# A cross network on one Trainium2 core: a semaphore lane for each transposed input tile, and the second layer's weights loaded behind the second group's rows

## Chip, cores and metric

The kernel runs on one core of a Trainium2 chip. The metric is the device time of one execution in microseconds (us); lower is better. The kernel before takes 488.22 us (median of 6 runs).

## The reference

```python
B, F, D, L = 16384, 26, 16, 6          # Din = F * D = 416; everything is bfloat16
def reference(x0, ws, bs):             # x0 [B, 416], ws [6, 416, 416], bs [6, 416]
    x = x0
    for l in range(L):
        x = x0 * (x @ ws[l] + bs[l]) + x
    return x
```

## The kernel before

The rows are cut into 8 groups of 2048. A group is held transposed, with features on the partitions: three tiles of 128 features (`t` = 0 to 2) and a "tail" of 32 features, which is loaded through a buffer `Tb` and copied from there to a place called `x03`. A job `(g, l)` is layer `l` of group `g`. It has three output tiles and a tail. For an output tile TensorE does 12 full matmuls (three input tiles, four chunks of 512 columns) and four short ones for the 32 tail features ("rows32"). ScalarE adds the bias, and VectorE multiplies by x0 and adds x.

Weights come in two parts: `wm` (384 rows) and `w3` (the last 32 rows, loaded four times to different partitions; the trace prints it as `w`, and I call the second layer's `w_1`). Nearly all these transfers are issued by SP, in the order of the program. Group 0 is not loaded by the transposing transfers but turned by TensorE, and its first layer (the "first job") runs while group 1 is loaded.

This is how a group is loaded; `lane` names the semaphore (the counter by which an engine learns that data has landed), and a reader of anything in a lane waits for the whole batch in it:

```python
def load_group(g):
    s = slot(g)
    rows = slice(g * GC, (g + 1) * GC)
    def turn(t):
        add("sp", lambda h: h.dma_start_transpose(
            x0s[s][:, t * GC:(t + 1) * GC], x0[rows, t * P:(t + 1) * P]),
            writes=[x0_tok(s, t, j) for j in range(NJ)], lane=f"x0_{s}", batch=g)
    turn(0)
    add("sp", lambda h: h.dma_start_transpose(Tb[:, :], x0[rows, D - P:D]), writes=["Tb"], lane="Tb", batch=g)
    turn(1)
    turn(2)
    for j in range(NJ):                                   # x03: copies out of Tb
        ...
# ... the start of the program
load_w3(0, "sp")
make_wbd(0)
load_wm(1, "sp")      # second layer's weights
load_w3(1, "sp")
load_group(1)         # second group's rows
load_wm(2, "sp")
load_w3(2, "sp")
```

And this is the order in which TensorE meets what was loaded, right after the first job:

```
first job (0,0), ending in its tails      -> VectorE later writes x3, the new tail of group 0
(1,0) tile 0: 12 full matmuls             needs tiles 0, 1, 2 of group 1, in this order
(1,0) tile 0: 4 short matmuls             needs x03 of group 1
(0,1) tile 0: 4 short matmuls             needs w_1 and x3      <- important below
(0,1) tile 0: 12 full matmuls             needs wm of layer 1
(1,0) tile 1, then the tails of (0,1) and (1,0)
```

Of the kernel before, what the change touches and what calls it, by code (L numbers as in the profile page):

```python
# [21 lines left out]
class Program:  # L22
# [12 lines left out]
    def add(self, eng, fn, reads=(), writes=(), lane=None, batch=None, hold=False, release=False):  # L35
        op = Op(eng, fn, lane, batch)
        deps = {}
        if eng == "pool":
            writes = list(writes) + ["pool"]
        for t in reads:  # L40
            w = self.writer.get(t)
            if w is not None:
                deps[id(w)] = (w, True)
        for t in writes:
            w = self.writer.get(t)
            if w is not None:
                deps[id(w)] = (w, True)
            for r in self.readers.get(t, ()):
                if id(r) not in deps:
                    deps[id(r)] = (r, False)  # L50
        for d, raw in deps.values():
            if d.lane is None and d.eng == eng and lane is None and (eng == "pe" or not raw):
                continue
            op.deps.append(d)
        for t in reads:
            self.readers.setdefault(t, []).append(op)
        for t in writes:
            self.writer[t] = op
            self.readers[t] = []
        if eng == "dve":  # L60
            if hold:
                self.flush()
                self.held = op
            else:
                self.queue[eng].append(op)
                if release:
                    self.flush()
        else:
            self.queue[eng].append(op)
        if lane is not None:  # L70
            batches = self.lanes.setdefault(lane, [])
            if not batches or batches[-1][0] != batch:
                batches.append((batch, []))
            batches[-1][1].append(op)
        return op
# [123 lines left out]
def bass_standalone__cross_network_dcn__recsys_kernel(  # L199
# [9 lines left out]
    NJ = 4  # L209
# [48 lines left out]
    def x0_tok(s, t, j):  # L258
        return ("x0", s, t, j)
# [7 lines left out]
    def slot(g):  # L267
        return g % NX0
# [12 lines left out]
    def load_wm(l, eng):  # L281
        add(eng, lambda h: h.dma_start(wm[l][:, :, :], ws[l, 0:NT * P, :].rearrange("(t p) f -> p t f", p=P)),
            writes=[("wm", l)], lane=f"wm{l}", batch=0)

    def load_w3(l, eng):
        for j in range(NJ):
            add(eng, lambda h, j=j: h.dma_start(w3[l][j * T32:(j + 1) * T32, :], ws[l, NT * P:D, :]),  # L287
                writes=[("w3", l, j)], lane=f"w3{l}", batch=0)

    def make_wbd(l):  # L290
        add("pool", lambda h: h.memset(wbd[l][:, :], 0.0), writes=[("wbd", l)])
        for j in range(NJ):
            q = slice(j * T32, (j + 1) * T32)
            add("pool", lambda h, q=q: h.tensor_copy(wbd[l][q, q], w3[l][q, NT * P:D]),  # L294
                reads=[("w3", l, j)], writes=[("wbd", l)])

    def load_group(g):
        s = slot(g)
        rows = slice(g * GC, (g + 1) * GC)
        def turn(t):  # L300
            add("sp", lambda h: h.dma_start_transpose(  # L301
                x0s[s][:, t * GC:(t + 1) * GC], x0[rows, t * P:(t + 1) * P]),
                writes=[x0_tok(s, t, j) for j in range(NJ)], lane=f"x0_{s}", batch=g)

        turn(0)
        add("sp", lambda h: h.dma_start_transpose(Tb[:, :], x0[rows, D - P:D]),  # L306
            writes=["Tb"], lane="Tb", batch=g)
        turn(1)
        turn(2)
        for j in range(NJ):  # L310
            q = slice(j * T32, (j + 1) * T32)
            add("sp", lambda h, q=q, j=j: h.dma_start(x0s[s][q, XW:XW + CH], Tb[P - T32:P, j * CH:(j + 1) * CH]),
                reads=["Tb"], writes=[("x03q", s, j)], lane=f"x03_{s}", batch=g)
# [26 lines left out]
    def done_with(g, l):  # L340
        users[(g, l)] = users.get((g, l), 0) + 1
        if users[(g, l)] < 2:
            return
        if l > 0:
            free_x.append(xset[(g, l)])
            free_3.append(xtail[(g, l)])
        if l == L - 1:
            output(g)
            if g == 3:
                load_last()  # L350
            if 4 < g + NX0 <= LAST:
                load_group(g + NX0)
# [136 lines left out]
        load_nat(j, 0, KK)  # L489
    load_w3(0, "sp")  # L490
    make_wbd(0)
    load_wm(1, "sp")
    load_w3(1, "sp")
    load_group(1)
    load_wm(2, "sp")
    load_w3(2, "sp")
    make_wbd(1)
# [165 lines left out]
    def start_job(g, l):  # L663
        started.add((g, l))
        xset[(g, l + 1)] = free_x.pop(0)
        if (g, l) in W_LOAD:
            load_wm(W_LOAD[(g, l)], "sp")
            load_w3(W_LOAD[(g, l)], "sp")
            make_wbd(W_LOAD[(g, l)])
        if (g, l) in G_LOAD:  # L670
            load_group(G_LOAD[(g, l)])
# [48 lines left out]
    g, l = LAST, L - 1  # L720
# [158 lines left out]
```

## Time and profile before

| | before |
|---|---|
| time, median of 6 runs | 488.22 us (488.06 to 488.44) |
| the profiled run | 488.65 us, span 486.5 us |
| TensorE busy | 472.3 us, 97% of the span |
| TensorE's largest wait for a load | 1.9 us, once, near 20.5 us |

The profile's page gives, for each engine, busy time, share of the span and number of instructions:

```profile
PE 472.3 (97%) x3199; PEld 202.7 (42%) x3253; DVE 407.2 (84%) x713; ACT 343.1 (71%) x372; POOL 16.4 (3%) x44
```

The view of waits of TensorE in the kernel before lists what ended its idle time: us in total, times, longest us. Two of its lines: (The second is the start-up, before TensorE has anything to work with.)

```profile
PE ps L423 <- DMA x<-in_x_dram: 1.9, 1, 1.9
PE ps L503 <- POOL ident L467: 1.8, 1, 1.8
```

The view has one more wait on a load, of 0.4 us near 7.6 us, so the wait of 1.9 us is nearly all there is to gain here. TensorE's own order of time, in the kernel before, shows where it lies. Columns: start in us, duration in us, engine, line, what is done, count, and in brackets the idle time before and what ended it. L453 ends the first tails, L423 are full matmuls, L435 the short ones, L448 the second tails.

```profile
20.07 0.39 PE L453 MATMUL ps<-x,wbd 128*32 128x512 bf16 x4
22.39 2.54 PE L423 MATMUL ps<-x,wm 128*128 128x512 bf16 x11 [1.93 <-DMA x<-in_x_dram]
24.86 0.61 PE L435 MATMUL ps<-x,w 32*128 32x512 bf16 x8
25.40 5.35 PE L423 MATMUL ps<-x,wm 128*128 128x512 bf16 x24
...
31.01 0.83 PE L448 MATMUL ps<-x,wm 128*32 128x512 bf16 x12
```

The chain of waits of the kernel before (start us, us, what) shows what held that load (pieces of 0.04 us between these, called `issue`, are left out here and below). `SPq` is the issuing of a transfer by SP; the landing is the `DMA` piece.

```profile
7.82 0.42 SPq L287
8.29 3.06 SPq L301
11.39 2.99 SPq L306
14.43 3.25 SPq L301
17.73 4.39 DMA x<-in_x_dram
```

Line L287 issues w_1, line L301 the three tiles of group 1, line L306 the buffer `Tb`. The last tile lands at 22.1 us (17.73 + 4.39). Tile 0 landed at 14.8 and tile 1 at 19.9 us (start of the issue plus the time to landing, of each transfer by itself), but with one lane TensorE can't tell.

### The profile page before, as it was taken

Reading aid. Unit: us, or ns where it says so; the run is one execution under the profiler, and the core shown is the slowest. Engines: PE = TensorE matmul, PEld = TensorE weight load, DVE = VectorE, ACT = ScalarE, POOL = GpSimd, SP = SyncE. Lnnn points to the kernel's source line nnn. Section 1 sums busy time; section 2 is a strip of 40 time slices with the busy share of each in tenths; the row PEclk is TensorE's granted clock in tenths of the full one; section 3 lists DMA queues with packets and bytes.
Section 4 is the critical chain, followed back from the end, with each engine's and each line's share of the span. In section 5 each row is a group of like instructions: output and inputs, shape, how many; then the busy total and the mean of one; then the engine's idle time right before and its main releaser. Section 6 shows DMA issues by size and latency. Waiting matters only on the chain.

```text
span 486.5 us, 8047 instructions
## 1 busy us (share of the span) xinstructions
PE 472.3 (97%) x3199; PEld 202.7 (42%) x3253; DVE 407.2 (84%) x713; ACT 343.1 (71%) x372; POOL 16.4 (3%) x44
## 2 busy tenths in 40 slices
PE   7899999999999999999999999999999999999996
PEld 6334444444444444444444444444444444444353
DVE  2878888888888888888889888988888888888887
ACT  4567777677677677766767767767777767777775
POOL 1033000000000000000000000000000000000000
PEclk9999999999999999999999999999999999999999
DMA  9897990000001397269209911850000137027277
GB/s 235 166 195 169 170 156 1 0 1 0 2 1 37 67 237 127 44 141 232 50 9 193 225 39 33 212 179 1 1 1 1 23 68 193 0 44 165 78 156 263
DMA packets 126249, 47.65 MB, mean 98 GB/s; under 512 B 107002, under 2 KB 124804, under 8 KB 126212
## 3 DMA queue, kind: packets, MB, share of 16 engines
q1 hardware_dynamic: 125656, 46.71, 43.5%
q8 instruction: 25, 0.41, 0.4%
q10 hardware_dynamic: 556, 0.43, 0.3%
q14 instruction: 12, 0.10, 0.1%
HBM read 5.97 MB, written 13.63 MB: 40 GB/s over the span
## 4 chain that ended last, share of the span: by engine, by line
PE 91%; SPq 3%; ACT 2%; issue 2%; DMA 1%; DVE 1%; DVEq 0%
PE ps L423 73%; PE ps L435 8%; PE ps L448 6%; PE ps L453 2%; PE ps L767 1%; SPq L301 1%; DMA x<-in_x_dram 1%; SPq L287 1%; ACT tw L382 1%; SPq L306 1%; ACT x L795 1%; SPq L478 0%; ACT x L759 0%; PE ps L778 0%; DVE x L396 0%
## 5 line engine op out<-in xcount | busy, mean ns | idle before, releaser
L382 ACT ACTIVATE tw<-ps,bias 128x1024 bf16<-128x1024 f32 (+1 forms) x295 | 299.8, 1071 | 128.9 <-PE ps L435 107.5
L423 PE MATMUL ps<-x,wm 128*128 128x512 bf16 x1638 | 371.9, 379 | 7.4 <-issue 3.7
L423 PEld LDWEIGHTS ps<-x,wm 128*128 128x128 bf16 x1692 | 158.9, 98 | 215.2 <-issue 28.3
L391 DVE TENSOR_TENSOR tw<-tw,x 128x1024 bf16<-128x1024 bf16 (+1 forms) x285 | 193.8, 686 | 63.9 <-ACT tw L382 63.6
L396 DVE TENSOR_TENSOR x<-tw,x 128x1024 bf16<-128x1024 bf16 (+1 forms) x285 | 182.3, 680 | 0.0
L435 PE MATMUL ps<-x,w 32*128 32x512 bf16 x564 | 44.3, 380 | 0.0
L448 PE MATMUL ps<-x,wm 128*32 128x512 bf16 x564 | 38.7, 380 | 0.0
L409 ACT ACTIVATE ts<-ps,bias 128x512 bf16<-128x512 f32 x47 | 28.8, 701 | 0.0
L435 PEld LDWEIGHTS ps<-x,w 32*128 32x128 bf16 x564 | 9.0, 92 | 33.1 <-issue 33.1
L448 PEld LDWEIGHTS ps<-x,wm 128*32 128x32 bf16 x564 | 13.8, 96 | 15.7 <-issue 2.9
L609 POOL COPY ost<-ot 128x512 bf16<-128x512 bf16 x7 | 4.8, 686 | 413.1 <-DMA ot<-x 413.1
L413 DVE TENSOR_TENSOR x<-ts,x 128x512 bf16<-128x512 bf16 x47 | 18.6, 420 | 0.0
L411 DVE TENSOR_TENSOR ts<-ts,x 128x512 bf16<-128x512 bf16 x47 | 18.6, 419 | 0.0
L453 PE MATMUL ps<-x,wbd 128*32 128x512 bf16 x188 | 18.3, 379 | 0.0
L294 POOL COPY wbd<-w 32x32 bf16<-32x32 bf16 x24 | 9.4, 392 | 35.9 <-DMA w<-in_ws_dram 34.7
L767 PE MATMUL ps<-wm,x 128*128 128x416 bf16 x48 | 9.4, 341 | 0.0
L536 DVE COPY x<-ps 128x512 bf16<-128x512 bf16 x4 | 1.7, 425 | 8.5 <-PE ps L528 8.5
L795 ACT ACTIVATE x<-ps 128x416 bf16<-128x416 f32 x15 | 7.4, 530 | 1.3 <-PE ps L767 1.2
L533 ACT ACTIVATE x<-ps 128x512 bf16<-128x512 bf16 x8 | 4.3, 594 | 4.6 <-PE ps L523 4.6
L453 PEld LDWEIGHTS ps<-x,wbd 128*32 128x32 bf16 x188 | 5.0, 97 | 5.1
L767 PEld LDWEIGHTS ps<-wm,x 128*128 128x128 bf16 x48 | 5.1, 115 | 3.8 <-issue 1.4
L797 DVE TENSOR_TENSOR x<-x,x 128x416 bf16<-128x416 bf16 x15 | 5.5, 371 | 1.1 <-ACT x L795 1.0
(37 smaller groups left out, 48.2 us busy)
## 6 DMA issues: line engine op xcount, KB each, us to landing
out_dram<-ost SPq DMA_DIRECT2D x7, 1664.0 KB, 6.8
x<-in_x_dram SPq DMA_DIRECT2D x7, 416.0 KB, 7.4
wm<-in_ws_dram SPq DMA_DIRECT2D x5, 312.0 KB, 3.2
x<-Tb SPq DMA_DIRECT2D x28, 32.0 KB, 2.2
out_dram<-x SPq DMA_DIRECT2D x1, 832.0 KB, 3.6
w<-in_ws_dram SPq DMA_DIRECT2D x24, 26.0 KB, 2.4
x<-in_x_dram SPq DMA_DIRECT2D x2, 208.0 KB, 3.1
out_dram<-x SPq DMA_DIRECT2D x1, 416.0 KB, 2.5
```

Source lines behind the costliest of these rows:

```text
L382: add("act", lambda h, a=a, w=w, b0=b0: h.activation(tw[r][:, a * CH:(a + w) * CH], psum[:, b0 * CH:(b0 + w) * CH], ACT_F.Identity, bias=b ...
L391: add("dve", lambda h, a=a, e=e: h.tensor_tensor(tw[r][:, a * CH:e * CH], tw[r][:, a * CH:e * CH], x0s[s0][:, i * GC + a * CH:i * GC + e * ...
L396: add("dve", lambda h, a=a, e=e: h.tensor_tensor(xs[so][:, i * GC + a * CH:i * GC + e * CH], tw[r][:, a * CH:e * CH], src(i, a, e), ALU.ad ...
L409: add("act", lambda h: h.activation(ts[r][:, :], bank(b), ACT_F.Identity, bias=bias[:, 3, l:l + 1], scale=1.0), reads=[("ps", b), "bias"], ...
L411: add("dve", lambda h: h.tensor_tensor(ts[r][:, :], ts[r][:, :], x0s[s0][:, XW:XW + CH], ALU.mult), reads=[("ts", r)] + x03_toks(s0), writ ...
L413: add("dve", lambda h: h.tensor_tensor(x3s[so][:, :], ts[r][:, :], src, ALU.add), reads=[("ts", r)] + stok, writes=[("x3", so)], hold=True)
L423: add("pe", lambda h, t=t, j=j: h.matmul(bank(banks[j]), wm[l][:, t, ecols], src(t, j, j + 1), start=(first and t == 0), stop=(not first a ...
L435: add("pe", lambda h, q=q, j=j: h.matmul(bank(banks[j]), w3[l][q, ecols], src[q, :], start=first, stop=not first, tile_position=(j * T32, 0)),
L448: add("pe", lambda h, t=t, j=j, src=src, l=l, b=b: h.matmul(bank(b, j * T32, (j + 1) * T32), wm[l][:, t, NT * P:D], src(t, j, j + 1), star ...
L453: add("pe", lambda h, j=j, s3=s3, l=l, b=b: h.matmul(bank(b, j * T32, (j + 1) * T32), wbd[l][:, j * T32:(j + 1) * T32], s3, start=False, s ...
L767: add("pe", lambda h, t=t: h.matmul(bank(b, n=D), xcol(t, j, kk), wm[l][:, t, :], start=(first and t == 0), stop=(not first and t == NT - 1)),
L795: add("act", lambda h: h.activation(o, bank(b, n=D), ACT_F.Copy), reads=[("ps", b)], writes=extra + [("on", j, kk)])
```

## The change

It has two parts. Each tile gets a lane of its own, so that TensorE can begin with tile 0 while tile 2 is on its way. And the second layer's weights no longer go ahead of the second group's rows: `wm` goes behind the three tiles and w_1 behind the x03 copies.

```diff
-    def load_group(g):
+    def load_group(g, between=lambda: None):
@@
-                writes=[x0_tok(s, t, j) for j in range(NJ)], lane=f"x0_{s}", batch=g)
+                writes=[x0_tok(s, t, j) for j in range(NJ)], lane=f"x0_{s}_{t}", batch=g)
@@
         turn(1)
         turn(2)
+        between()
@@
-    load_wm(1, "sp")
+    load_group(1, lambda: load_wm(1, "sp"))
     load_w3(1, "sp")
-    load_group(1)
     load_wm(2, "sp")
```

## The prediction

> **What bounds the kernel now.** The page's engine table gives TensorE 97% of a 486.5 us span, and the chain of waits is 91% TensorE. Its only large wait on a load is 1.9 us "PE ps L423 <- DMA x<-in_x_dram", once: from 20.46 us (end of the first tail, L453) to 22.39 us the first matmul of the second group waits. The chain of waits before that is SP's issue queue: row loads, first-layer tails, the second layer's weights (5.83, 0.49 us) and its four tail loads (6.37, 1.88 us), four transposes (8.29 to 20.05 us).
>
> The four transposes land (source-line view) at 14.8 (tile 0), 17.8 (Tb), 19.9 (tile 1) and 22.1 us (tile 2). With one lane of one batch, the first matmul waits for tile 2, though it needs only tile 0. The Trainium skill, "DMA: Bandwidth & Descriptors", section on why a DMA increments its semaphore by 16, says only a full count tells that all data landed; the old wait is therefore on all three.
>
> **What the change does.** (a) Lanes: tile 0 would be usable at once at 20.46; eight matmuls (0.22 us each) later, about 22.2, tile 2 has landed. This alone removes nearly the whole wait. (b) Order: about 2.46 us of issuing (0.53 + 1.92) moves from ahead of the transposes to behind them. Tile 2 should land near 19.7 to 20.3, before TensorE asks. Either part suffices; they aren't additive. No work is added or removed; a few more TensorE waits on full semaphores I count as nothing.
>
> **What it puts in the way.** The order view shows TensorE's next waits after the group's first 12 matmuls: the second group's tail rows (x03), then tail weights w_1 and, in the same wait, VectorE's x3 of the first job; then wm1.
> - TensorE reaches the x03 rows near 23.1, w_1/x3 near 23.35 (12 x 0.22 + 4 x 0.07 after 20.46). Before, the w_1 matmuls started near 25.15.
> - VectorE is busy without a gap from 16.9 to 24.33 us and writes x3 last (L413, 23.91 + 0.42). The removed wait doesn't gate it, so TensorE can't start the w_1 matmuls before about 24.4.
> - w_1 is now issued after x03, some 20.7 to 22.6 us, as SP's issuing in sum is unchanged; at 1.9 to 2.4 us to landing it arrives at 24.2 to 24.9. wm1 lands near 21.5, early enough.
>
> So of the 1.93 us about 1.2 to 1.6 returns as a new wait at L435 on w_1 or x3, and 0.3 to 0.75 us is gained. From then on TensorE is bound (59.2 to 59.4 of each 60 us), loads have over 5 us of slack, and the gain should carry to the end unchanged.
>
> **Predicted:** 487.75 us (gain 0.6), 8 in 10 range 487.0 to 488.4. Faster by over 2%: 0.005; within 2%: 0.99; slower by over 2%: 0.005.
>
> **What would show it.** Right: the wait at 20.46 is gone, x_1's matmuls start by 20.7; a new TensorE wait of 1 to 1.5 us stands before the w_1 matmuls of L435, ended by VectorE's L413 or the w_1 load at 24.4 to 24.9; wait list without the 1.9 us; from 60 us on all is shifted by a constant 0.3 to 0.75 us. Wrong: no such wait and a shift of about 1.9 us; or transposes that land no earlier.
>
> **What would make it wrong.** Transposes issued at 5.83 may meet the first group's loads still in flight (DMA share 1.02 in 6 to 9 us) and delay the first job, eating the gain; SP's issue of transposes may be held by a full queue (3.06 us for the first, against 1.89 us at 27.6), pushing w_1 past 25.1 and the gain to zero.

## The result, and the profile after

The changed kernel took 487.94 us (median of 6, 487.71 to 488.44) against 488.22 us. The ratio is 0.9995, with a 95% interval of 0.9983 to 1.0008. The time was inside the predicted range. The gain isn't clear of noise.

The profiles differ more than the times do: span 485.8 against 486.5 us. One line was added, so L423 became L424, L435 became L436 and so on. Two lines of the waits of TensorE in the changed kernel:

```profile
PE ps L503 <- POOL ident L468: 1.8, 1, 1.8
PE ps L436 <- DMA w<-in_ws_dram: 1.1, 1, 1.1
```

The wait for the rows is gone, and there is a new one, for w_1. TensorE's order of time in the changed kernel shows it:

```profile
19.91 0.39 PE L454 MATMUL ps<-x,wbd 128*32 128x512 bf16 x4
20.45 2.54 PE L424 MATMUL ps<-x,wm 128*128 128x512 bf16 x11 [0.16 <-ACT tw L383]
22.93 0.39 PE L436 MATMUL ps<-x,w 32*128 32x512 bf16 x4
24.41 0.40 PE L436 MATMUL ps<-x,w 32*128 32x512 bf16 x4 [1.09 <-DMA w<-in_ws_dram]
24.74 5.35 PE L424 MATMUL ps<-x,wm 128*128 128x512 bf16 x24
...
30.35 0.83 PE L449 MATMUL ps<-x,wm 128*32 128x512 bf16 x12
```

TensorE starts on group 1 at 20.45 instead of 22.39 us, 1.94 us earlier, but reaches the second tails only 0.66 us earlier (30.35 against 31.01). And right behind the load stands VectorE. Its order of time in the changed kernel has x3 as its last instruction of the first job:

```profile
23.29 0.42 DVE L412 TENSOR_TENSOR ts<-ts,x 128x512 bf16<-128x512 bf16 x1
23.74 0.43 DVE L414 TENSOR_TENSOR x<-ts,x 128x512 bf16<-128x512 bf16 x1
```

The w_1 load landed at 24.27 us (22.61 + 1.66 in the chain of waits) and x3 was written at 24.17 us. Both are needed by the matmuls that began at 24.41 us.

The chain of waits of the changed kernel shows that the transposes were issued earlier, but not by as much as the loads taken away from ahead of them:

```profile
5.52 4.25 SPq L301
9.82 2.94 SPq L306
12.80 2.68 SPq L301
15.53 2.29 SPq L301
17.86 0.59 SPq L282
```

The first transpose now takes 4.25 us to issue, against 3.06 us before. It starts 2.77 us earlier and ends 1.58 us earlier (9.77 against 11.35).

### The profile page after: what moved, and what is told of

It is laid out like the page before. It is cut to its first block, busy times and chain, and to the rows that moved or that the text cites. A ratio compares the mean times of both kernels' runs of the same rounds, so it can differ in the third digit from the quotient of the medians.

```text
span 485.8 us, 8047 instructions
## 1 busy us (share of the span) xinstructions
PE 472.8 (97%) x3199; PEld 203.2 (42%) x3253; DVE 407.2 (84%) x713; ACT 343.2 (71%) x372; POOL 16.0 (3%) x44
## 4 chain that ended last, share of the span: by engine, by line
PE 91%; SPq 4%; ACT 2%; issue 2%; DVE 1%; DMA 0%; DVEq 0%
PE ps L424 73%; PE ps L436 8%; PE ps L449 6%; PE ps L454 2%; SPq L301 2%; PE ps L767 1%; SPq L287 1%; ACT tw L383 1%; SPq L306 1%; ACT x L795 1%; SPq L313 0%; SPq L479 0%; DMA w<-in_ws_dram 0%; ACT x L759 0%; PE ps L778 0%
## 5 line engine op out<-in xcount | busy, mean ns | idle before, releaser
L424 PE MATMUL ps<-x,wm 128*128 128x512 bf16 x1638 | 371.9, 379 | 5.6 <-issue 3.7
L424 PEld LDWEIGHTS ps<-x,wm 128*128 128x128 bf16 x1692 | 158.8, 98 | 213.3 <-issue 28.5
L436 PE MATMUL ps<-x,w 32*128 32x512 bf16 x564 | 44.5, 380 | 1.1 <-DMA w<-in_ws_dram 1.1
L436 PEld LDWEIGHTS ps<-x,w 32*128 32x128 bf16 x564 | 9.2, 92 | 34.5 <-issue 33.1
L454 PE MATMUL ps<-x,wbd 128*32 128x512 bf16 x188 | 18.3, 379 | 0.0
L454 PEld LDWEIGHTS ps<-x,wbd 128*32 128x32 bf16 x188 | 5.0, 97 | 5.1
```

The source lines that it names most:

```text
L424: add("pe", lambda h, t=t, j=j: h.matmul(bank(banks[j]), wm[l][:, t, ecols], src(t, j, j + 1), start=(first and t == 0), stop=(not first a ...
L436: add("pe", lambda h, q=q, j=j: h.matmul(bank(banks[j]), w3[l][q, ecols], src[q, :], start=first, stop=not first, tile_position=(j * T32, 0)),
L454: add("pe", lambda h, j=j, s3=s3, l=l, b=b: h.matmul(bank(b, j * T32, (j + 1) * T32), wbd[l][:, j * T32:(j + 1) * T32], s3, start=False, s ...
```

## The experiments

Before the single runs, one account that holds for all of them. In each profile I read three numbers from TensorE's order of time: when the first tails end (start plus duration of the L453 or L454 group, 20.07 + 0.39 = 20.46 us in the kernel before), when the second tails start (31.01 us), and the **stage** between them (10.55 us). The last column is the time of that same run less the start of the second tails.

| profiled run | time us | first tails end | second tails start | stage | rest |
|---|---|---|---|---|---|
| before, first profile | 488.65 | 20.46 | 31.01 | 10.55 | 457.64 |
| before, second (before_p2) | 487.61 | 20.15 | 30.01 | 9.86 | 457.60 |
| before, third (before_p3) | 489.85 | 19.70 | 32.22 | 12.52 | 457.63 |
| changed, first profile | 487.98 | 20.30 | 30.35 | 10.05 | 457.63 |
| changed, second (after_again) | 487.34 | 19.84 | 29.72 | 9.88 | 457.62 |
| changed, third (after_p3) | 487.69 | 20.22 | 30.09 | 9.87 | 457.60 |
| lanes_only | 487.80 | 20.31 | 30.18 | 9.87 | 457.62 |
| order_only | 487.88 | 20.42 | 30.28 | 9.86 | 457.60 |
| tails_early | 487.85 | 20.38 | 30.25 | 9.87 | 457.60 |
| rows_last | 486.96 | 20.33 | 29.33 | 9.00 | 457.63 |
| tile_swap | 486.75 | 20.36 | 29.14 | 8.78 | 457.61 |
| tile_swap_lanes | 487.28 | 20.87 | 29.65 | 8.78 | 457.63 |
| tile_swap_before | 487.24 | 20.85 | 29.63 | 8.78 | 457.61 |
| w1_later | 491.42 | 20.19 | 33.76 | 13.57 | 457.66 |

The rest is 457.60 to 457.66 us in all fourteen. So whatever these kernels differ in has happened by the second tails, and nothing is given back later. What remains is when the first job ends, which varies between runs of one and the same code (19.70, 20.15, 20.46 for the kernel before), and the stage.

**My theory:** after the load wait, x3 by VectorE and the w_1 load are the next things that TensorE needs, both near 24.2 us, so most of a shorter load wait comes back as a wait there. **Rivals:** that only one of the two parts of the change gains; that the late w_1 load alone is the new limit; that the wait of 1.9 us in the first profile is typical of the kernel before.

### lanes_only, order_only: one part of the change at a time

lanes_only is the kernel before with the lanes split; order_only is the changed kernel with `lane=f"x0_{s}"` again.

```diff
# lanes_only, against the kernel before
-                writes=[...], lane=f"x0_{s}", batch=g)
+                writes=[...], lane=f"x0_{s}_{t}", batch=g)
# order_only, against the changed kernel
-                writes=[...], lane=f"x0_{s}_{t}", batch=g)
+                writes=[...], lane=f"x0_{s}", batch=g)
```

> Kernel before with only the semaphore lanes split; issue order untouched. My theory (after the load wait, x3 by VectorE at about 24.2 to 24.4 us and the w_1 load are the next things TensorE needs, so either part alone gives the whole gain): TensorE starts on the second group by 20.7 us although tile 2 lands only near 22.1; a short wait for the x03 rows (last lands near 23.8 us) and one for x3 follow; the w_1 matmuls start at 24.4 to 24.6 us; span shorter than before by 0.5 to 0.75 us, level with the changed kernel within 0.2 us. Rival (the new load order is what gains): no gain, under 0.2 us.

> The changed kernel with one lane for all three tiles again, so only the order of loading changes. My theory: tile 2 lands near 20.5 us, within 0.2 us of when TensorE asks; w_1 matmuls start at 24.4 us as in the changed kernel; gain 0.5 to 0.75 us against before, so the two parts are not additive. Rival (lanes are what gains): the wait at 20.46 stays near 1.9 us, no gain.

In both, the wait for the rows is gone, and TensorE waits for VectorE's x3 instead. TensorE's order of time in lanes_only, and then in order_only:

```profile
20.24 2.76 PE L423 MATMUL ps<-x,wm 128*128 128x512 bf16 x12
22.93 0.40 PE L435 MATMUL ps<-x,w 32*128 32x512 bf16 x4
24.24 0.39 PE L435 MATMUL ps<-x,w 32*128 32x512 bf16 x4 [0.91 <-DVE x L413]
```

```profile
20.35 2.76 PE L424 MATMUL ps<-x,wm 128*128 128x512 bf16 x12
23.04 0.40 PE L436 MATMUL ps<-x,w 32*128 32x512 bf16 x4
24.34 0.40 PE L436 MATMUL ps<-x,w 32*128 32x512 bf16 x4 [0.91 <-DVE x L414]
```

The stage is 9.87 and 9.86 us: with either part alone TensorE meets the same limit, so the rival that only one part gains doesn't hold. The stage by itself doesn't prove that each part was needed, for before_p2 (below) reaches 9.86 us with neither. What shows that the lanes work is that TensorE began at 20.24 us in lanes_only, while tile 2 landed near 21.5 us; in order_only tile 2 landed near 19.5 us (15.2 + 4.3), before TensorE asked. The separate wait for x03 that I had expected in lanes_only did not show. In time, lanes_only was 487.42 us (ratio 0.9989, interval 0.9975 to 1.0003) and order_only 487.84 us (0.9997, 0.9985 to 1.001), beside 488.00 us for the kernel before. The intervals overlap; the runs don't rank the two.

### after_again: the changed kernel with more rounds

No edit.

> The changed kernel unedited, to get its ratio with more rounds. My theory from the traces: 0.66 us shorter, ratio 0.9986. Rival from the first three rounds' medians: 0.28 us, ratio 0.9994.

487.88 us, ratio 0.9998 (0.9985 to 1.0011), with a stage of 9.88 us. The 0.66 us of the profiles was not confirmed in the times; nor can 0.28 us be told from nothing. Why the profiles show more than the times is what before_p2 and before_p3 are for.

### tails_early: w_1 early again

```diff
-    load_group(1, lambda: load_wm(1, "sp"))
     load_w3(1, "sp")
+    load_group(1, lambda: load_wm(1, "sp"))
```

> The changed kernel with the four w_1 loads put ahead of the transposes again, and only wm1 behind them. w_1 then lands before 15 us. If x3 from VectorE is a second limit right behind the w_1 load (my theory), the w_1 matmuls still start at 24.2 to 24.5 us, the wait stays about 0.9 to 1.1 us and is put down to VectorE, and the time equals the changed kernel's within 0.25 us. If the w_1 load alone binds (rival), the wait goes and the span falls by a further 0.9 to 1.1 us.

TensorE's order of time in tails_early:

```profile
24.31 0.40 PE L436 MATMUL ps<-x,w 32*128 32x512 bf16 x4 [0.91 <-DVE x L414]
```

Its wait stayed 0.9 us and was put down to VectorE; the stage was 9.87 us, and the time 487.63 us (0.9992, 0.9979 to 1.0004). So w_1 is not the only limit: with w_1 early, x3 holds TensorE at the same place. In the first profile of the changed kernel the load came 0.10 us after x3, and the stage was 0.18 us longer than here.

### rows_last and tile_swap: take the need for x3 and w_1 out of the way

In rows_last the four short matmuls of (0,1) tile 0 come after its 12 full ones. In tile_swap the second tile of group 1's first layer goes ahead of (0,1) tile 0, so that x3 and w_1 are asked for some 5 us later. Both edit the changed kernel:

```diff
# rows_last
     mode[len(items) - 1] = "RF"
+    mode[0] = mode[1] = "F1"
# tile_swap
-    where[((1, 0), 1)] = where.pop(((1, 0), 0))
-    tiles = [((1, 0), 0), ((0, 1), 0), ((1, 0), 1), ...
+    where[((0, 1), 0)] = where.pop(((1, 0), 0))
+    tiles = [((1, 0), 0), ((1, 0), 1), ((0, 1), 0), ...
```

> The changed kernel; in the first tile of the first group's second layer TensorE does the 12 full-height matmuls first and the four short ones that need x3 and w_1 last. My theory (x3 and w_1 hold TensorE for 0.9 to 1.1 us after the change): that wait is gone, the short matmuls run near 25.8 us long after both are there, and the span falls by 0.6 to 0.95 us against the changed kernel (one more switch between full and short matmuls costs up to 0.25 us). If VectorE's whole evacuation holds TensorE rather than x3 alone, the wait comes back at once on VectorE or ScalarE and the gain is under 0.3 us.

> The changed kernel with the second group's second tile moved ahead of the first group's second layer, so that x3 and w_1 are asked for some 5 us later. My theory: no TensorE wait over 0.4 us between 19 and 34 us, span 0.8 to 1.0 us under the changed kernel's, together about 1.1 to 1.6 us under before, and a smaller spread between runs, since the w_1 load has slack again. Rival (another limit right behind): under 0.3 us.

TensorE's order of time in tile_swap has no idle time over 0.16 us in this stage:

```profile
20.52 2.54 PE L424 MATMUL ps<-x,wm 128*128 128x512 bf16 x11 [0.16 <-ACT tw L383]
22.99 0.61 PE L436 MATMUL ps<-x,w 32*128 32x512 bf16 x8
23.53 5.35 PE L424 MATMUL ps<-x,wm 128*128 128x512 bf16 x24
28.82 0.40 PE L436 MATMUL ps<-x,w 32*128 32x512 bf16 x4
29.14 0.83 PE L449 MATMUL ps<-x,wm 128*32 128x512 bf16 x12
```

The stage is 8.78 us, 1.09 us under the 9.87 of the kernels that wait for x3. In rows_last it is 9.00 us; the 0.22 us more go with its one more switch between full and short matmuls. Nothing else took the place of the wait. The times are 486.96 us for rows_last (ratio 0.9979, 0.9967 to 0.9992) and 486.63 us for tile_swap (0.9968, 0.9956 to 0.9981), beside 487.99 us for the kernel before. These are the only kernels here, with tile_swap_lanes below, whose interval lies wholly below 1, and tile_swap has the lowest median of all kernels run. One caution: unedited code moved by 0.42 us against its own yardstick (before_p2, below), about as much as the near end of the interval of rows_last (0.39 us), so its time alone is weak; that of tile_swap (0.9 us at the near end) is not. The smaller spread that I had expected in tile_swap isn't shown: its five runs span 0.87 us. The stages and the missing wait, with the time of tile_swap, settle that x3 and w_1 held the changed kernel.

### tile_swap_lanes, tile_swap_before: the same swap without the new load order, and without both

> The kernel before with split lanes and the same swap of tiles, old load order. The x03 rows land about 1 us later than in the changed kernel and are now asked for near 23 us. My theory: the wait for x3 goes, at most 0.5 us of waiting for x03 appears, span 1.0 to 1.6 us under before. If the new load order is needed once x3 is out of the way, this one is slower than the same swap on the changed kernel by 0.3 to 0.8 us.

> Control: the kernel before with only the swap of tiles, one lane, old load order. My theory: the wait for tile 2 of the second group (1.4 to 1.9 us at about 20.4 us) stays whole, and in it the x3 wait is hidden, so the swap gives nothing: within 0.3 us of before. If the swap is good by itself, it is 0.8 us or more faster.

tile_swap_lanes had the same stage, 8.78 us, and took 487.01 us (0.9975, 0.9961 to 0.9988). The x03 rows were in time. The expectation's alternative, that the new load order is needed now, isn't shown: it was 0.38 us slower than tile_swap in the median, but its stage was the same, and its profile is later only because the first tails ended later.

The control, tile_swap_before, missed its expectation. The load wait should have stayed; in this profile there was none. TensorE's order of time in tile_swap_before:

```profile
20.46 0.39 PE L453 MATMUL ps<-x,wbd 128*32 128x512 bf16 x4
21.01 2.54 PE L423 MATMUL ps<-x,wm 128*128 128x512 bf16 x11 [0.16 <-ACT tw L382]
```

It has one lane and the old load order, and the rows were there when TensorE asked: the last transpose was issued near 15.8 us, against 17.73 us in the first profile of before, and the first tails ended 0.39 us later (20.85 against 20.46). So the wait of 1.93 us isn't a fixed property of the kernel before. It depends on how the first job and the transposes fall against each other in a run. The profile is of the fastest of this kernel's five runs (487.24 us; the others took 487.38 to 488.10), so the wait may well stand in the others. The median time was 487.40 us (0.9989, 0.9976 to 1.0001), which is not clear of noise.

### before_p2, before_p3, after_p3: how much does the load wait vary?

No edits: the kernel before twice and the changed kernel once, for more profiles.

> The kernel before, unedited, for a second profile. From the end of the first tails to the start of the second tails TensorE took 10.55 us in the first profile of before, 9.87 in four kernels that wait for x3 and 8.78 where it waits for nothing. My theory: the stage is 8.78 us plus the longer of the load wait w (its excess over the usual 0.16) and 1.09 us for x3, and w varies from run to run with the landing of tile 2, so this profile shows a stage between 9.87 and 10.55; the first profile, the slowest of all runs of before, overstated w. Rival: the wait is 1.9 us in every run and the stage 10.5 us again.

> The same again, a third profile: stage between 9.87 and 10.55 us by my theory, equal to 8.78 plus the longer of tile 2's excess wait and 1.09; 10.5 by the rival.

> The changed kernel, unedited, for a third profile. My theory: stage 9.87 us where x3 ends the wait, up to 0.5 us more where the w_1 load lands later than x3 (10.05 in the first profile); ratio 0.999 to 1.000 to before. Rival (the profiles' 0.66 us is typical): ratio 0.9986 or lower.

In before_p2 the rows came a little late. TensorE's order of time:

```profile
20.88 2.54 PE L423 MATMUL ps<-x,wm 128*128 128x512 bf16 x11 [0.73 <-ACT tw L382]
23.35 0.39 PE L435 MATMUL ps<-x,w 32*128 32x512 bf16 x4
24.07 0.39 PE L435 MATMUL ps<-x,w 32*128 32x512 bf16 x4 [0.33 <-DVE x L413]
```

The wait of 0.73 us is put down to ScalarE, but the same profile puts the weight load ahead of that matmul down to the rows (1.0 us, "DMA x<-in_x_dram"), and tile 2 landed near 20.6 us. The load wait only ate into the wait for x3: the stage is 9.86 us, as in the kernels with no load wait at all. In a run like this the change has nothing to gain.

before_p3 is the other extreme, and showed something that I had not expected. TensorE's order of time:

```profile
19.31 0.39 PE L453 MATMUL ps<-x,wbd 128*32 128x512 bf16 x4
21.91 4.22 PE L423 MATMUL ps<-x,wm 128*128 128x512 bf16 x11 [2.22 <-DMA x<-in_x_dram]
26.07 0.61 PE L435 MATMUL ps<-x,w 32*128 32x512 bf16 x8
```

The same 11 matmuls took 4.22 us instead of 2.54 us. The table of stretches of before_p3 (stretch, its length, TensorE's busy time and matmuls, granted clock, which is the share of its full clock that TensorE was given, DMA share, GB/s) tells why:

```profile
19.70:21.90 2.20, 0.00 (x0) 1.00 0.79 179
21.90:22.90 1.00, 0.99 (x3) 0.56 0.23 60
22.90:23.90 1.00, 1.00 (x3) 0.50 0.66 171
23.90:24.90 1.00, 1.00 (x4) 0.50 0.73 223
24.90:25.90 1.00, 1.00 (x5) 0.73 0.46 83
25.90:26.90 1.00, 1.00 (x12) 1.00 0.94 295
```

After 2.22 us without work TensorE was granted half its clock for 3.41 us (22.03 to 25.44), which cost 4.22 - 2.54 = 1.68 us on top of the wait. After the 1.93 us of the first profile of before, the clock stayed at 1.00.

The length of the wait is not all that decides. In these traces the granted clock changes only on a grid of 3.41 us: the half clock lasted 3.41 us here and in w1_later, and the full clock before it 5 times and 6 times as long (17.07 and 20.48 us). So I ask how busy TensorE was in the 3.41 us before a change. In before_p3 it was 35% (1.20 us in 18.61 to 22.03) and in w1_later 17% (0.58 us in 23.30 to 26.71), and the clock fell; in the first profile of before, the stretch on the same grid (18.60 to 22.01) was 55% busy (1.86 us), because the last 0.38 us of the wait fell into the next one, and the clock stayed. That is a reading of three profiles, and no run tested it.

The stage of the kernel before is then 8.78 us, plus the longer of the load wait (less the usual 0.16) and 1.09, plus 1.68 where the clock falls. This gives 8.78 + 1.77 = 10.55 for the first profile (measured 10.55), 8.78 + 1.09 = 9.87 for the second (9.86), and 8.78 + 2.06 + 1.68 = 12.52 for the third (12.52). My expectation for the third, a stage of at most 10.55 us, failed, because it had no term for the clock. (The 1.68 us are taken from that same profile, so the third sum is an account and not a test.)

In time, before_p2 took 487.81 us, ratio 0.9992 (0.9979 to 1.0004), although it is the same code as the kernel that it is divided by; after_p3 took 487.71 us, ratio 0.9991 (0.9978 to 1.0003). Identical code moves by as much as the change does; in this one job the means of the changed kernel (487.77) and of before_p2 (487.81) are 0.04 us apart. before_p3 was a single run (489.85 us, mean clock 0.995, state unknown), so it tells what can happen, not how often. None of the 33 timed runs of the kernel before that served as the yardstick was above 488.59 us.

### w1_later: make w_1 later on purpose

```diff
-    load_w3(1, "sp")
     load_wm(2, "sp")
     load_w3(2, "sp")
+    load_w3(1, "sp")
```

> The changed kernel with the third layer's five weight loads (2.4 us of issuing) put ahead of the second layer's tail loads w_1. If w_1 lands within 0.3 us of x3 in the changed kernel (my theory), the wait before the w_1 matmuls grows to 3.0 to 3.4 us, is put down to the load, the stage is about 12.2 us and the span is 2.0 to 2.5 us longer than the changed kernel's. If w_1 has a microsecond or more of slack behind x3, it is 1.2 us longer at most.

The wait grew to 2.92 us, and the w_1 matmuls began at 26.13 us, 1.72 us after those of the first profile of the changed kernel. TensorE's order of time:

```profile
22.82 0.40 PE L436 MATMUL ps<-x,w 32*128 32x512 bf16 x4
26.13 0.40 PE L436 MATMUL ps<-x,w 32*128 32x512 bf16 x4 [2.92 <-DVE tw L392]
26.46 7.04 PE L424 MATMUL ps<-x,wm 128*128 128x512 bf16 x24
```

The name in brackets misleads: x3, the only thing from VectorE that these matmuls need, was written at 24.06 us in this profile, while the last w_1 transfers were issued at 23.9 to 24.4 us and took 1.6 to 1.8 us to land, so until about 26.0 us. GpSimd, which waits for the same load alone, began at 26.12 us. A wait for several semaphores is put down to one of them, and that can be the wrong one. The 24 full matmuls behind it took 7.04 instead of 5.35 us: the half clock again, 0.50 in the profile from 26.7 to 30.1 us, worth 1.69 us. It fell 0.58 us after TensorE had work again, so the clock during the wait itself tells nothing. The stage, 13.57 us, would be 11.88 without it; I had expected 12.2. The time was 491.33 us in the median (ratio 1.0055, 1.004 to 1.007), 3.6 us above after_p3, where I expected 2.0 to 2.5. The four runs were 491.42, 491.24, 491.61 and 489.86 us, with mean clocks of 0.995, 0.995, 0.994 and 0.998. The last of them, whose mean clock was that of after_p3 (0.998), is 2.15 us above after_p3, within what I expected; it has no profile. So w_1 has next to no slack behind x3 in the changed kernel, and a wait of two to three microseconds can be charged twice.

## Why the prediction was right, point by point

- *The wait for the rows goes; TensorE starts on group 1 by 20.7 us.* Right: 20.45, 20.24 and 20.35 us in the changed kernel, lanes_only and order_only. "Either part suffices" fits too: 9.87 and 9.86 us, though before_p2 got to 9.86 with neither.
- *1.2 to 1.6 us returns as a wait before the w_1 matmuls, ended by x3 or w_1 at 24.4 to 24.9 us.* Right in kind and nearly in size: 1.09 us of idle time, ended at 24.41 us, in the first profile, and 0.92 and 0.90 us, ended by x3 at 23.78 and 24.15 us, in the other two. Of the 1.94 us by which TensorE starts earlier, 1.28 was lost again (1.94 - 0.66). That x3 is a limit of its own is shown by tails_early; that the two together are the limit, by rows_last and tile_swap.
- *The w_1 load arrives at 24.2 to 24.9 us.* Right: 24.27 us. The risk that "SP's issue of transposes may be held by a full queue" came true in part: the first transpose took 4.25 us to issue instead of 3.06, and SP was done with w_1 at 23.03 us, 0.43 us later than my 22.6. That the loads still in flight caused it is not shown. tails_early fits a hold that ends near 10 us whenever the issue begins: there the first transpose was issued 2.05 us later (7.57 against 5.52), took 2.51 us, and was done only 0.31 us later (10.08 against 9.77). The other risk, that the earlier transposes delay the first job, did not show: with the new order the first tails ended at 19.84 to 20.42 us, with the old at 19.70 to 20.87. w_1 also landed faster, in 1.66 us.
- *The shift carries to the end unchanged.* Right, and to 0.06 us: the rest column.
- *A gain of 0.6 us, 487.75 us.* The range held, and 487.94 us is 0.19 us off, but the range is a weak test: the 488.22 us of the kernel before lie in it too, so no gain at all would have passed. The mechanism was right; that the number came so near is partly luck. The size was right for the two first profiles (0.66 us) but not for the times. Pooled, the changed kernel's 16 runs average 487.90 us, and the yardstick's 33 runs of the kernel before 488.12 us: 0.22 us, no more than identical code moved (0.42 us between the means of before_p2, 487.81, and its yardstick, 488.23). The step that was too large is the load wait: I took 1.93 us from one profile, of a run (488.65 us) slower than all 33, as a property of the kernel. In other runs it was 0.73, 2.22 or, with the tiles swapped, nothing.
- *Not foreseen:* that after a load wait 0.29 us longer than this one (2.22 us in before_p3) TensorE was granted half its clock. In none of its three profiles did the changed kernel wait for the rows, so it may save more in a rare run; how rare, these runs don't say.

The end of the first job varies by up to 0.76 us between runs of the same code (19.70 to 20.46 us), and the profiles show most of why. The first matmuls of 128x128 took 314 ns each, and from a certain time on 219 ns, and that time, where the record of the full clock also begins, varied from run to run: 4.96 us in before_p3, 6.00 in before_p2, 7.84 in tile_swap_before. (The view of stretches prints 1.00 before it, so it is read from the matmuls.) The same eight matmuls took 0.62 us in before_p3 (at 5.94 us) and 1.03 us in tile_swap_before (at 6.43 us). Over all profiles but the first of before, the first tails ended at 19.70 to 19.84 us where that time was 4.8 to 5.0 us, at 20.15 to 20.42 where it was 6.0 to 6.9, and at 20.85 and 20.87 where it was 7.8. The first profile of before (4.94 us, but 20.46) is the exception; it alone waited 0.43 us for a row load at 7.6 us. So in tile_swap_before a late full clock is part of why no load wait was left. No run changed the clock on purpose.

What stays open is whether lanes_only is in truth a little faster than the changed kernel, as its median hints (487.42 against 487.88 us).

## What to carry to other kernels

Before removing a wait, list what the waiting engine needs next and when each of those things is ready: of a wait of 1.93 us only 0.66 us was won here, because VectorE's x3, ready near 24.2 us, didn't depend on that load at all. The work that is worth moving then is the work that asks for the latest result: the change together with a swap of two tiles of TensorE's order gave 1.36 us (487.99 to 486.63; identical code moved by 0.42), and the change alone nothing that the times could resolve. And take the size of a wait on a load from several profiles, not one; if it comes near two microseconds on TensorE, look at the granted clock after it.

## What the Trainium skill lacked or had wrong

- "TensorE: Matmul & The Clock Gate", section "Part 1: The HAM clock gate", puts the fall to half clock after at least one idle window of about 3.4 us, and says that the window runs freely. Here 2.22 us of idle time were enough in one run and 2.92 us in another, while 1.93 us were not in a third. The length of the window agrees: the half clock lasted 3.41 us, and the clock changed on a grid of that length. What differs is "idle": a wait of 2.22 us can't fill a window of 3.4 us, and the windows before the two falls were 35% and 17% busy. With 55% the clock stayed. So a writer who takes a wait under 3.4 us as safe is misled by these runs. What the page says of the two clock levels agrees: 0.50, then 1.00, at a cost of 1.68 and 1.69 us.
- "Perfetto Trace Analysis", section "DMA Instruction — HWDGE (DVE, Sync)", says that a transfer's slice is its issue, and the moving of data isn't in it. That agrees (the third transpose was issued in 2.29 us and landed 5.0 us after its issue began). The page doesn't say how much the issue itself varies: a transposing transfer of one tile (line L301) took 1.89 us to issue at 27.6 us in the kernel before, and 4.25 us at 5.5 us in the changed one.
- "DMA: Bandwidth & Descriptors", section "Why a DMA increments its semaphore by 16 and not by 1", explains why a shared lane must be waited for in full. Splitting the lane worked as it implies: TensorE began on tile 0 at 20.24 us in lanes_only, while tile 2 landed near 21.5 us (16.8 + 4.7). What it was worth in time here is less than identical code moved; there is nothing to correct on that page.
